# A fused Mamba-2 scan and low-rank mixer on one core: state updates, copies of y and joins become steps of their own, and the order of issue after the sixth pair's second transpose is another one

## The chip, the core and the metric

The kernel runs on 1 core of one Trainium2 chip. The metric is device time in microseconds (us), the median of several executions. Before the change it is 226.42 us (3 runs, 226.41 to 228.46). The profile beside it is one execution, whose span is 224.7 us: from the first to the last instruction of the program that the profiler saw. The 1.7 us between the two lie around the span (start and end of an execution).

The engines are named as in the profile: PE is TensorE's matmul side and PEld its weight loads, DVE is VectorE, ACT is ScalarE, POOL is GpSimd, and SP issues the DMAs. Each engine takes its instructions in the order in which the program has them.

## The reference

Four batches of 768 tokens, eight heads of 32 channels and a state of 16. A scan in chunks of 32 gives y; y of all heads side by side is the input (768 x 256) of a mixer over tokens and channels.

```python
for c in range(nc):                      # chunks of 32 tokens
    cum = np.cumsum(la, axis=-1)
    L = np.exp(cum[:, :, :, None] - cum[:, :, None, :]) * causal
    M = np.einsum('bhin,bhjn->bhij', Cc, Bc) * L
    y_intra = np.einsum('bhij,bhjd->bhid', M, xc)
    y_inter = np.einsum('bhin,bhnd->bhid', Cc, state) * np.exp(cum)[:, :, :, None]
    y[:, :, sl] = y_intra + y_inter
    decay_from_j = np.exp(cum[:, :, -1:] - cum)
    Bx = np.einsum('bhjn,bhjd->bhjnd', Bc, xc) * decay_from_j[..., None, None]
    state = decay_full[:, :, None, None] * state + np.sum(Bx, axis=2)
...
x = y.transpose(0, 2, 1, 3).reshape(B, S, H * D)
h = x.transpose(0, 2, 1) @ U @ V                   # over the tokens, rank 32
u = x + h.transpose(0, 2, 1)
out = u + np.maximum(u @ w_ch1, 0.0) @ w_ch2       # 256 -> 1024 -> 256
```

The weights U, V, w_ch1 and w_ch2 are 64-bit floats in memory; the kernel reads them as words and makes fp32 of them.

## The kernel before

The scan is cut into twelve pairs of 128-token blocks: pair k is block pair k % 3 of batch k // 3. The mixer works per batch b, on halves j of 384 tokens. There is no scheduler: the string PLAN (lines 36 to 73) is the order of issue, word by word, and `follow` (line 859) calls one function for each word. Each function issues its instructions on their engines at once, so the string fixes the order on every engine's queue.

Words of the scan, with the pair's number k:

- `L` loads B, C (three DMAs) and x (two). Words `B X w L` hold their first DMA until the last DVE instruction issued so far has ended (line 864).
- `P` scales B and C (one DVE instruction, tile BC). `T`, twice per pair, gives its four transposes on PE into a bank "w"; the second `T` ends with three ACT copies (tiles T and Cm, lines 484 to 490).
- `g` is the Gram product into all four banks "x" and "z" (line 511); `m` and `M` mask the two x banks and the two z banks (two DVE instructions each, tile M).
- `s` multiplies B and x for the new states into both banks "w" (line 543); `u` makes the running states (up to four DVE instructions, tile S, each needing the one before) and, on POOL, their masked form Sm (line 569).
- `i`, `n`, `j` add up y in the two banks "y" (lines 613 and 635); `y` copies both banks to yT (two ACT copies, line 648); `t` turns yT back to tokens (four transposes into a bank "w" and one copy, line 656).

Words of the mixer, with batch b and half j:

- `p`, `q` project over the tokens (bank "w", tiles pT and ps; lines 679 and 687); `a` adds V's part to yT (line 697); `S` splits u in three parts (tile u: one ACT, two DVE instructions of 128x768).
- `f b.j.m` multiplies column block m of w_ch1 with two of the parts (four matmuls into a bank "x" for even m, "z" for odd m) and scales it on ACT; `e` adds the third part (two matmuls), then the ACT gives the rounded value (line 759); `h` takes the remainder on DVE and so frees the bank. For odd m, `h` goes on with `joined`: one DVE instruction of 128x768 that makes a third operand out of the pair of blocks m-1 and m.
- `d b.j.k.n` is piece n of the second product for token block k of a half: four matmuls of 256 columns, six pieces a block, into one bank whose tag depends on k ("x", "z", "x"; "y" for the last three halves, line 18). Pieces 0 and 1 read the rounded values, 2 and 3 the remainders, 4 and 5 the joined operand. After piece 5 come one more matmul with ps, a DVE addition to ytok and the DMA to the output. Batch 0 has four plain pieces of two fp32 matmuls with two passes each; its first product is `U b.j.m`.
- `c` and `R` convert and split the weights (DVE and ACT).

PSUM holds two banks of each of the four tags "w", "x", "z" and "y". A new use of a bank waits for the instruction that read the old contents. In the traces, operand names are u,w for `f` and `e`, w,words for pieces 0 to 3 of `d`, w2c,words for pieces 4 and 5 and for batch 0, ps,Vs for the last matmul of an output.

Of the kernel before, what the change touches and what calls it, by code (L numbers as in the profile page):

```python
# [10 lines left out]
FP32 = mybir.dt.float32  # L11
# [23 lines left out]
    'b0.0 b0.1 b0.2 x0.0 x0.1 b1.0 b1.1 b1.2 ')  # L35
PLAN = (
# [37 lines left out]


@with_exitstack
def kernel(
# [28 lines left out]
    P = 128  # L106
# [33 lines left out]
            n -= m  # L140

    def bank(tag, *dims):
        t = psum.tile([P, *dims], FP32, tag=tag, name=tag, bufs=BANKS[tag])
        return t

    ctx.enter_context(tc.manual_schedule())

# [72 lines left out]
    w1all = mix.tile([P, NQ, NCB, W], FP32, tag="u", name="w1f", bufs=1)  # L220
    w1f = [w1all[:, c] for c in range(NQ)]
    w2 = [const.tile([P, NM, DM], FP32R, name=f"w2{i}") for i in range(2)]
    weights = []
    w2f, w2b = {}, {}

    def w2c(n, dtype):
# [4 lines left out]
    def words_of(dst):  # L231
        p, i, j = dst.shape
        t = raw.tile([P, 2 * WCOLS], INT32, tag="words", name="words", bufs=NWORDS)
        weights.append((dst, t[:p, :2 * i * j]))
        return t[:p, :2 * i * j]

    def each(parts, *index):
        return [part[index] for part in parts]

    def load_words(dst, src):  # L240

        p, i, j = dst.shape
        t = words_of(dst)
        begin(out=t.rearrange("p (i j) -> p i j", i=i), in_=src)

    U2, V2, w12, w22 = (w.bitcast(INT32) for w in (moe_U, moe_V, moe_w_ch1, moe_w_ch2))
# [4 lines left out]

    def load_v():
        own["UV"] = words_of(UV)
        for q in range(4):
            begin(out=own["UV"][ts(q, Q), 2 * NC * RK:], in_=V2[:, ts(q, 2 * NC * RK)])

# [3 lines left out]

    def load_w(n):
        if n < 2:
            if n == 0:
                own["w"] = words_of(w1f[0])
                weights.pop()
            dst, t = w1f[0][:, :, ts(n, P)], own["w"][:, ts(n, 2 * NCB * P)]
            weights.append((dst, t))
            begin(out=t.rearrange("p (i j) -> p i j", i=NCB),
                  in_=w13[:, :, ts(n, 2 * P)])
        elif n <= NQ:  # L270
            load_words(w1f[n - 1], w13[:, :, ts(n - 1, 2 * quarter)])
        else:
            m = 2 * (n - NQ - 1)
            load_words(w2c(n - NQ - 1, FP32), w22[m * P:(m + 2) * P].rearrange(
                "(m p) d -> p m d", p=P))

    def load(k):
# [271 lines left out]
    def update(k, c=0, n=2):  # L549

        b, q = pairs[k]
        s = st[k]
        if c == 0:
            s["S"] = att.tile([P, 4, 2 * D], FP32, tag="S", name="S")
            s["Sm"] = att.tile([P, 4, 2, D], FP32, tag="Sm", name="Sm", bufs=3)
        own = chunks(k, c, n)
        for i in own:
            j = 4 * q + i
            new, add = s["S"][:, i], s["A"][i % 2][:, i // 2]
            if j == 0:  # L560
                vector.tensor_copy(out=new, in_=add)
            else:
                vector.scalar_tensor_tensor(
                    out=new, in0=st["S", b], scalar=kept[:, b, j - 1, None], in1=add,
                    op0=ALU.mult, op1=ALU.add)
            st["S", b] = new
            st["Sm", b, j + 1] = s["Sm"][:, i].rearrange("p s d -> p (s d)")
        sl = slice(own[0], own[-1] + 1)
        nc.gpsimd.tensor_tensor(  # L569
            out=s["Sm"][:, sl], in0=s["S"][:, sl].rearrange("p i (s d) -> p i s d", s=2),  # L570
            in1=own2[:, b, 4 * q + sl.start:4 * q + sl.stop, :, None].to_broadcast(
                [P, len(own), 2, D]), op=ALU.mult)

    def apart(k):

# [62 lines left out]
                            stop=True, skip_group_check=True)  # L638
                        behind.setdefault(k, []).append(product)

    def yout(k):
        b, q = pairs[k]
        if q == 0 and b:
            yT[b] = mix.tile([P, NCB, S], FP32, tag="yT", name="yT")
            ytok[b] = mix.tile([P, NC, DM], FP32, tag="ytok", name="ytok")
        yp = yT[b][:, :, ts(q, 2 * P)].rearrange("p g (c v i) -> p g c v i", c=2, v=2)
        for p in range(2):
            nc.scalar.copy(out=yp[:, :, :, p], in_=st[k]["y"][p])  # L648

    def ytokening(k, tag="w"):  # L650

# [17 lines left out]
    def mixer(b):  # L669
# [91 lines left out]
        def third(j, m):  # L761
# [2 lines left out]
            vector.scalar_tensor_tensor(  # L764
                out=far[:, m % 2], in0=gs["t", j, m], scalar=0.0,
                in1=near[:, m % 2].bitcast(FP32), op0=ALU.max, op1=ALU.subtract)
            if m % 2:
                joined(near, far, both)

        def down(j, k, n):  # L770

# [18 lines left out]
            if n == pieces - 1:  # L790
# [3 lines left out]
                nc.sync.dma_start(out=out[b, ts(c, P)], in_=o)  # L794

        us, gs, gT = {}, {}, {}
        return SimpleNamespace(p=project, q=parted, a=added, S=split, f=first, e=second, h=third,
                               d=down, U=plain)


# [46 lines left out]
    def ytokens_kept(k):  # L847
        next(turns["O", k])

    scans = dict(P=prep, T=turned, g=gram, s=state, m=lambda k: mask(k, (0, 1)),  # L850
                 M=lambda k: mask(k, (2, 3)), u=update, i=lambda k: inter(k, 0), n=intra,
                 j=lambda k: inter(k, 1), y=yout, t=ytokens, L=load, Q=lambda k, c: prep(k, c, 1),
                 O=ytokens_of, o=ytokens_kept,
                 V=lambda k, c, v: turn(k, c, 1, "wx"[v // 2], vector if v % 2 else None))
# [54 lines left out]
```

## Time and profile before

| | before |
|---|---|
| median of 3 runs | 226.42 us |
| span of the profiled execution | 224.7 us |
| DVE busy | 156.7 us (70%), 329 instructions |
| ACT busy | 114.3 us (51%), 261 instructions |
| POOL busy | 14.3 us (6%), 37 instructions |
| PE: last matmul starts | 220.86 us |
| second transpose of the sixth pair (t5) starts | 64.71 us |
| granted TensorE clock, every slice | full |

All times below are microseconds from the span's start. A busy share of PE is no measure of how fast it goes: a matmul counts as busy until its modelled end, and matmuls overlap. What tells is the distance from the start of one to the start of the next, and so the start of one group to the start of the next.

### The profile page before, as it was taken

To read this page: it belongs to the slowest core of one execution; us is meant where nothing else is said; L and a number is where in the kernel's file an instruction comes from. 1 tells how busy PE (TensorE), PEld (TensorE's weight loads), DVE (VectorE), ACT (ScalarE), POOL (GpSimd) and SP (SyncE) were. 2 spreads that over 40 slices of the span, in tenths; PEclk is the share of its full clock that TensorE was granted. 3 is DMA by queue.
4 is the path that set the end of the run, shared out by engine and by line. 5 is a ranking of instruction groups with operands and counts; after the bars stand their busy time and mean duration, and the time that the engine had idled before them with its cause. 6 is when DMAs were issued, how large, how long until landed. Compare 5 with 4: busy or idle time off the path is not lost.

```text
span 224.7 us, 7010 instructions
## 1 busy us (share of the span) xinstructions
PE 216.0 (96%) x3012; PEld 182.8 (81%) x3012; DVE 156.7 (70%) x329; ACT 114.3 (51%) x261; POOL 14.3 (6%) x37
## 2 busy tenths in 40 slices
PE   7888989999999999999999999999999999999993
PEld 4656655656668898987999898887998999999993
DVE  4776878899998866969717785758437964764921
ACT  3334946856994346334453632475237545655410
POOL 3021010012100000202101000100000000000000
PEclk9999999999999999999999999999999999999999
DMA  6997799788645203600002602000020000100011
GB/s 88 127 111 144 132 130 287 139 163 230 92 65 72 51 23 59 84 23 26 3 26 48 96 0 73 3 3 3 1 71 1 0 0 26 47 0 28 32 38 47
DMA packets 69518, 14.56 MB, mean 65 GB/s; under 512 B 63792, under 2 KB 67696, under 8 KB 69488
## 3 DMA queue, kind: packets, MB, share of 16 engines
q1 hardware_dynamic: 69488, 14.13, 34.6%
q8 instruction: 23, 0.38, 0.7%
q14 instruction: 7, 0.06, 0.1%
HBM read 10.98 MB, written 3.15 MB: 63 GB/s over the span
## 4 chain that ended last, share of the span: by engine, by line
PE 91%; DVE 2%; DMA 2%; SPq 1%; issue 1%; POOL 0%; ACT 0%; POOLq 0%; DVEq 0%
PE x L725 31%; PE z L725 24%; PE y L725 12%; PE y L613 4%; PE y L635 3%; PE w L480 3%; PE x L511 3%; PE w L656 2%; DMA bc<-in_B_dram 2%; PE w L543 2%; PE z L511 2%; PE x L138 1%; SPq L185 1%; PE w L679 1%; PE w L138 1%
## 5 line engine op out<-in xcount | busy, mean ns | idle before, releaser
L159 DVE SCALAR_TENSOR_TENSOR words<-words 128x768 fp32r<-128x768 f32 (+6 forms) x44 | 34.6, 806 | 1.9 <-ACT words L416 0.6
L725 PE MATMUL z<-u,w 128*128 128x384 f32 x144 | 34.0, 350 | 0.0
L725 PE MATMUL x<-u,w 128*128 128x384 f32 x144 | 33.1, 348 | 0.0
L730 ACT ACTIVATE x<-x 128x384 f32<-128x384 f32 (+1 forms) x30 | 13.6, 452 | 25.3 <-PE x L725 25.1
L725 PEld LDWEIGHTS z<-u,w 128*128 128x128 f32 x144 | 24.5, 188 | 1.3 <-DVE words L159 0.2
L725 PEld LDWEIGHTS x<-u,w 128*128 128x128 f32 x144 | 24.0, 188 | 1.3 <-ACT x L730 0.6
L159 DVE SCALAR_TENSOR_TENSOR words<-x,words 128x384 fp32r<-128x384 f32 x24 | 13.2, 555 | 16.4 <-ACT words L759 13.7
L725 PE MATMUL x<-w2c,words 128*128 128x256 f32 x112 | 22.5, 338 | 0.0
L730 ACT ACTIVATE z<-z 128x384 f32<-128x384 f32 (+1 forms) x27 | 12.5, 463 | 14.1 <-PE z L725 13.6
L725 PEld LDWEIGHTS x<-w2c,words 128*128 128x128 f32 x112 | 18.2, 189 | 1.3
L725 PE MATMUL y<-w,words 128*128 128x256 f32 x144 | 19.1, 282 | 0.0
L725 PEld LDWEIGHTS y<-w,words 128*128 128x128 f32 x144 | 18.5, 188 | 0.3 <-DVE ytok L159 0.3
L159 DVE SCALAR_TENSOR_TENSOR words<-z,words 128x384 fp32r<-128x384 f32 x24 | 13.2, 551 | 5.7 <-ACT words L759 5.7
L759 ACT ACTIVATE words<-x 128x384 fp32r<-128x384 f32 x24 | 11.6, 490 | 6.3 <-PE x L725 6.1
L759 ACT ACTIVATE words<-z 128x384 fp32r<-128x384 f32 x24 | 11.6, 491 | 4.9 <-PE z L725 4.8
L648 ACT COPY yT<-y 128x256 f32<-128x256 f32 x24 | 7.8, 384 | 10.9 <-PE y L613 10.7
L569 POOL TENSOR_TENSOR Sm<-S,own 128x256 f32<-128x256 f32 (+1 forms) x12 | 7.7, 644 | 87.5 <-DVE S L159 58.1
L159 DVE SCALAR_TENSOR_TENSOR S<-S,kept,w 128x64 f32<-128x64 f32 x40 | 11.2, 280 | 2.7 <-PE w L543 0.9
L613 PE MATMUL y<-T,Sm 32*64 32x64 f32 x352 | 12.4, 239 | 0.4 <-POOL Sm L569 0.3
L725 PE MATMUL x<-w,words 128*128 128x256 f32 x96 | 12.6, 282 | 0.0
L725 PEld LDWEIGHTS x<-w,words 128*128 128x128 f32 x96 | 12.0, 188 | 0.1
L511 PE MATMUL x<-Cm,T 32*64 32x128 f32 x192 | 11.0, 307 | 1.0 <-ACT Cm L490 0.7
(152 smaller groups left out, 400.5 us busy)
## 6 DMA issues: line engine op xcount, KB each, us to landing
words<-in_moe_w_ch_dram SPq DMA_DIRECT2D x7, 512.0 KB, 6.1
x<-in_x_dram SPq DMA_DIRECT2D x24, 128.0 KB, 3.7
out_dram<-ytok SPq DMA_DIRECT2D x24, 128.0 KB, 1.7
bc<-in_B_dram SPq DMA_DIRECT2D x24, 64.0 KB, 3.7
bc<-in_C_dram SPq DMA_DIRECT2D x12, 128.0 KB, 3.8
words<-in_moe_w_ch_dram SPq DMA_DIRECT2D x2, 256.0 KB, 4.5
words<-in_moe_V_dram SPq DMA_DIRECT2D x4, 48.0 KB, 3.1
words<-in_moe_U_dram SPq DMA_DIRECT2D x1, 192.0 KB, 3.5
```

The source lines that it names most:

```text
L138: nc.tensor.matmul(out=t[:, :m * w].rearrange("p (m i) -> p m i", i=w), lhsT=ident, rhs=ident[:, None, :w].to_broadcast([P, m, w]), start= ...
L159: self.last = call(*args, **kwargs)
L480: nc.tensor.transpose(out=tp[:, i, v], in_=s["BC"][:, i, c + v].rearrange("p h n -> p (h n)"), identity=ident)
L511: nc.tensor.matmul(out=g[r][cols, c], lhsT=s["T"][rows, 0, c, cols], rhs=s["Cm"][rows, :, :, ts(2 * c + p, Q)].rearrange("r v t i -> r v i ...
L543: nc.tensor.matmul(out=s["A"][p][ts(r, Q), v], lhsT=s["BC"][half, 0, v, 2 * r:2 * r + 2].rearrange("p h n -> p (h n)"), rhs=x_sb[k][half, ...
L569: nc.gpsimd.tensor_tensor(out=s["Sm"][:, sl], in0=s["S"][:, sl].rearrange("p i (s d) -> p i s d", s=2), in1=own2[:, b, 4 * q + sl.start:4 ...
L613: product = nc.tensor.matmul(out=y[p][ts(r % 2, H), r // 2, c], lhsT=own[ts(r, Q)], rhs=s["T"][ts(r, Q), 1, :, ts(2 * c + p, Q)].rearrange ...
L635: product = nc.tensor.matmul(out=y[p][ts(i, Q), n, c], lhsT=x_sb[k][half, c, h], rhs=s["M"][half, h // 2, c, h % 2], start=fresh(k, p, [i] ...
L648: nc.scalar.copy(out=yp[:, :, :, p], in_=st[k]["y"][p])
L725: nc.tensor.matmul(out=t, lhsT=lhsT, rhs=rhs, start=start, stop=True, skip_group_check=True)
L730: nc.scalar.activation(t, t, AF.Copy, scale=1.0 + EPS)
L759: nc.scalar.activation(gs[j, m // 2][0][:, m % 2], t, AF.Relu, scale=NEAR)
```

## The change

Three functions are cut. `yout` copies one bank of y at a time (`y k.p`). `update` takes one block of the pair at a time (`u k.c`); the POOL instruction is still one for the pair and comes with the second. `joined` is called by a word of its own, `J b.j.i`, no longer by `h`. The list of converted weights becomes a table by number, so that loads could be in any order. No instruction is added or taken away on any engine.

```diff
@@ update
-        sl = slice(own[0], own[-1] + 1)
+        if c + n < 2:
+            return
+        sl = slice(0, own[-1] + 1)
@@ yout
-    def yout(k):
+    def yout(k, p):
...
-        for p in range(2):
-            nc.scalar.copy(out=yp[:, :, :, p], in_=st[k]["y"][p])
+        nc.scalar.copy(out=yp[:, :, :, p], in_=st[k]["y"][p])
@@ third
-            if m % 2:
-                joined(near, far, both)
+
+        def fourth(j, n):
+
+            joined(*gs[j, n])
```

PLAN is the same up to `t5 m6` (pieces of `u` and `y` stand side by side there). What follows is in another order. Four places of it, the order of before above that of after:

```diff
-    'y5 U0.0.7 c8 U0.0.5 t5 m6 n6 R3 c9 c9 P8 c8 p1 R7 g7 m7 L9 i6 M7 T8 T8 c8 c8 q1 d0.0.2.0 '
-    'd0.0.2.1 U0.1.5 a1.1 R1 d0.0.2.2 d0.0.2.3 a1.0 d0.0.1.0 R3 d0.0.1.1 d0.0.1.2 d0.0.0.0 d0.0.0.1 '
+    'U0.0.5 t5 m6 c8 U0.1.5 L10 R5 P8 c8 T8 p1 n6 c8 i6 g7 m7 R1 M7 j6 T8 c9 q1 c9 d0.1.2.0 d0.1.2.1 '
+    'd0.0.1.0 d0.1.2.2 R7 d0.0.1.1 R3 a1.0 y6.1 d0.1.2.3 d0.0.0.0 R3 a1.1 S1.0 P10 d0.0.0.1 d0.0.0.2 '
...
-    'd0.1.1.2 d0.1.1.3 e1.0.4 e1.0.5 d0.1.2.1 d0.1.2.2 h1.0.4 h1.0.5 R6 d0.1.2.3 s8 j6 g8 y6 u8 s9 '
-    'm8 n7 i7 S1.1 f1.1.0 f1.1.2 j7 y7 u9 M8 t6 R5 e1.1.0 h1.1.0 n8 i8 T9 T9 t7 R5 d1.0.1.0 '
+    'h1.0.5 s7 u7.0 f1.0.4 d0.0.2.3 u7.1 f1.0.1 e1.0.4 J1.0.3 h1.0.4 f1.0.0 d0.1.1.2 L9 e1.0.1 '
+    'd0.1.0.0 y6.0 d0.1.0.1 R7 e1.0.0 h1.0.0 d0.1.1.3 h1.0.1 J1.0.2 d0.1.0.2 d0.1.0.3 n7 s8 i7 L11 '
+    'P9 u8.0 g8 M8 j7 m8 T9 S1.1 d1.0.1.0 d1.0.1.1 J1.0.0 T9 d1.0.2.0 f1.1.1 f1.1.0 y7.0 d1.0.2.1 '
...
-    'd1.1.0.5 d1.1.2.4 d1.1.2.5 d1.1.1.4 d1.1.1.5 T10 g9 m9 T10 T11 T11 M9 i9 n9 g10 m10 M10 j9 y9 '
-    's11 u11 i10 g11 m11 M11 n10 f2.0.4 a2.1 f2.0.3 f2.0.2 e2.0.4 h2.0.4 e2.0.3 e2.0.2 f2.0.7 '
-    'f2.0.6 h2.0.2 h2.0.3 f2.0.0 f2.0.1 e2.0.0 e2.0.7 e2.0.1 h2.0.0 h2.0.1 j10 y10 t9 e2.0.6 h2.0.6 '
-    'h2.0.7 f2.0.5 i11 n11 e2.0.5 h2.0.5 d2.0.1.0 d2.0.0.0 d2.0.0.1 d2.0.0.2 d2.0.0.3 d2.0.1.1 '
+    'd1.1.2.1 d1.1.2.2 d1.1.2.3 d1.1.0.4 d1.1.1.4 d1.1.2.4 d1.1.2.5 d1.1.1.5 d1.1.0.5 s10 g9 u10.0 '
+    'u10.1 T10 m9 T10 T11 M9 T11 i9 n9 g10 m10 j9 y9.0 M10 s11 y9.1 i10 u11.0 g11 M11 u11.1 m11 n10 '
+    'f2.0.7 a2.1 f2.0.2 e2.0.7 h2.0.7 f2.0.0 f2.0.3 e2.0.2 j10 h2.0.2 t9 e2.0.0 e2.0.3 y10.1 f2.0.4 '
+    'f2.0.5 h2.0.0 h2.0.3 f2.0.6 y10.0 f2.0.1 e2.0.5 e2.0.4 J2.0.1 e2.0.6 e2.0.1 i11 h2.0.5 h2.0.1 '
+    'h2.0.6 n11 t10 d2.0.1.0 d2.0.2.0 d2.0.2.1 d2.0.2.2 h2.0.4 S2.1 d2.0.1.1 J2.0.3 d2.0.2.3 f2.1.1 '
...
-    'h2.1.1 e2.1.2 h2.1.2 h2.1.3 f2.1.4 p3 e2.1.4 f2.1.5 f2.1.6 h2.1.4 e2.1.5 h2.1.5 q3 f2.1.7 '
+    'f2.1.3 d2.0.0.3 f2.1.6 e2.1.5 t11 e2.1.3 e2.1.6 h2.1.6 h2.1.3 J2.1.1 p3 d2.0.0.4 q3 f2.1.7 '
```

More of the change, by code (lines that the diff above doesn't have):

```diff
@@ L142, in bank @@
     def bank(tag, *dims):
-        t = psum.tile([P, *dims], FP32, tag=tag, name=tag, bufs=BANKS[tag])
-        return t
+        return psum.tile([P, *dims], FP32, tag=tag, name=tag, bufs=BANKS[tag])
     ctx.enter_context(tc.manual_schedule())
@@ L222 @@
     w2 = [const.tile([P, NM, DM], FP32R, name=f"w2{i}") for i in range(2)]
-    weights = []
+    weights = {}
     w2f, w2b = {}, {}
@@ L233, in words_of @@
         t = raw.tile([P, 2 * WCOLS], INT32, tag="words", name="words", bufs=NWORDS)
-        weights.append((dst, t[:p, :2 * i * j]))
         return t[:p, :2 * i * j]
@@ L238, in each, with load_words @@
         return [part[index] for part in parts]
-    def load_words(dst, src):
+    def load_words(n, dst, src):
         p, i, j = dst.shape
         t = words_of(dst)
+        weights[n] = dst, t
         begin(out=t.rearrange("p (i j) -> p i j", i=i), in_=src)
@@ L253, in load_v @@
         own["UV"] = words_of(UV)
+        weights[1] = UV, own["UV"]
         for q in range(4):
@@ L262, in load_w @@
         if n < 2:
-            if n == 0:
+            if "w" not in own:
                 own["w"] = words_of(w1f[0])
-                weights.pop()
             dst, t = w1f[0][:, :, ts(n, P)], own["w"][:, ts(n, 2 * NCB * P)]
-            weights.append((dst, t))
+            weights[2 * n] = dst, t
             begin(out=t.rearrange("p (i j) -> p i j", i=NCB),
@@ L270, in load_w @@
         elif n <= NQ:
-            load_words(w1f[n - 1], w13[:, :, ts(n - 1, 2 * quarter)])
+            load_words(n + 1, w1f[n - 1], w13[:, :, ts(n - 1, 2 * quarter)])
         else:
             m = 2 * (n - NQ - 1)
-            load_words(w2c(n - NQ - 1, FP32), w22[m * P:(m + 2) * P].rearrange(
+            load_words(n + 1, w2c(n - NQ - 1, FP32), w22[m * P:(m + 2) * P].rearrange(
                 "(m p) d -> p m d", p=P))
@@ L567, in update @@
             st["Sm", b, j + 1] = s["Sm"][:, i].rearrange("p s d -> p (s d)")
-        sl = slice(own[0], own[-1] + 1)
+        if c + n < 2:
+            return
+        sl = slice(0, own[-1] + 1)
         nc.gpsimd.tensor_tensor(
             out=s["Sm"][:, sl], in0=s["S"][:, sl].rearrange("p i (s d) -> p i s d", s=2),
-            in1=own2[:, b, 4 * q + sl.start:4 * q + sl.stop, :, None].to_broadcast(
-                [P, len(own), 2, D]), op=ALU.mult)
+            in1=own2[:, b, 4 * q:4 * q + sl.stop, :, None].to_broadcast(
+                [P, sl.stop, 2, D]), op=ALU.mult)
     def apart(k):
@@ L639, in intra @@
                         behind.setdefault(k, []).append(product)
-    def yout(k):
+    def yout(k, p):
         b, q = pairs[k]
-        if q == 0 and b:
+        if b not in yT:
             yT[b] = mix.tile([P, NCB, S], FP32, tag="yT", name="yT")
@@ L796, in mixer @@
         us, gs, gT = {}, {}, {}
-        return SimpleNamespace(p=project, q=parted, a=added, S=split, f=first, e=second, h=third,
+        return SimpleNamespace(p=project, q=parted, a=added, S=split, f=first, e=second, h=third, J=fourth,
                                d=down, U=plain)
@@ L850 @@
     scans = dict(P=prep, T=turned, g=gram, s=state, m=lambda k: mask(k, (0, 1)),
-                 M=lambda k: mask(k, (2, 3)), u=update, i=lambda k: inter(k, 0), n=intra,
+                 M=lambda k: mask(k, (2, 3)), u=lambda k, c: update(k, c, 1), i=lambda k: inter(k, 0), n=intra,
                  j=lambda k: inter(k, 1), y=yout, t=ytokens, L=load, Q=lambda k, c: prep(k, c, 1),
```

55 rows, old and new, of the table PLAN are left out of this document.

## The prediction

> **What bounds the kernel now.** I read the engines' busy times, the chain of waits by engine, and the timeline of PE, DVE and ACT from 64.71 us on, where the two orders part.
>
> ```profile
> PE 216.0 (96%) x3012; PEld 182.8 (81%) x3012; DVE 156.7 (70%) x329; ACT 114.3 (51%) x261; POOL 14.3 (6%) x37
> ...
> PE 91%; DVE 2%; DMA 2%; SPq 1%; issue 1%; POOL 0%; ACT 0%; POOLq 0%; DVEq 0%
> ```
>
> PE bounds it. As no instruction comes or goes, only time in which PE advances slower than it can is to be had. Its best rate, from PE's timeline:
>
> ```profile
> 130.21 1.58 PE L725 MATMUL z<-w,words 128*128 128x256 f32 x12
> 131.64 2.53 PE L725 MATMUL x<-w,words 128*128 128x256 f32 x20
> 134.00 0.40 PE L725 MATMUL x<-w2c,words 128*128 128x256 f32 x2
> ```
>
> 32 matmuls in 3.79 us: 0.118 each. In the same way 16 of 384 columns start from 191.42 to 194.19: 0.174 each. The small ones in these rows:
>
> ```profile
> 139.80 0.86 PE L635 MATMUL y<-M,x 64*32 64x64 f32 x64
> 140.59 0.35 PE L511 MATMUL x<-Cm,T 32*64 32x128 f32 x2
> ...
> 141.18 0.47 PE L613 MATMUL y<-T,Sm 32*64 32x64 f32 x12
> 141.58 0.53 PE L543 MATMUL w<-x,BC 64*32 64x64 f32 x24
> 142.15 0.57 PE L613 MATMUL y<-T,Sm 32*64 32x64 f32 x8
> ```
>
> `n` costs 0.79, `g` 0.59 and `i` or `j` 0.40 (start to next start); `s` 0.36 (101.21 to 101.57).
>
> By these prices I went through PE's groups from 64.71 on. Between 107.4 and 137.2 and from 156.3 to 211.6 they stand at their price. The losses: 0.2 at the start (an addition of V's part at 71.53 waits for ps, on DVE 71.05 to 71.48); 0.6 in stage 1 (100.8 to 107.4: `g8` 0.72, the mixed `s9`, `n7` 1.38, first products 1.59 for 1.48 and others); 1.7 in stage 2 (137.2 to 145.6, with its transposes: `g9` 1.08, `s11` 0.57, `j10` with `g11` 1.47 for 0.93, first products 0.80); 0.8 behind it (145.6 to 156.3: 6.74 for 6.26 from 145.57, 1.41 for 1.13 from 153.15, 0.46 for 0.35 at 155.79); 0.2 at 211.67. Together about 3.2 us, all that can go: 223.2 us.
>
> **Pieces.** `u`, `y` and `J` issue what was issued before, in smaller words: 0. POOL's one instruction a pair waits for the pair's last `u` as it did.
>
> **Start.** After puts `U0.1.5` ahead of `T8`, and `P8` ahead of `c9` on DVE; ps is then ready about 1 us before `a1.0` reads it. The wait goes: -0.2. `c9`'s DVE instruction (0.69) ends some 0.7 us before its reader; no new wait.
>
> **Loads.** `L9` moves from about 68 to 96 us, where its first DMA is held until the DVE instruction of `h1.0.4` ends, about 95.9. From the load at 87.09: its three issues take 0.39, 0.57 and 0.57 and the last lands 4.65 after the first issue, so about 100.7. `P9`, the DVE instruction that needs it, is due at about 102.1. Slack 1.4 us: 0. `L10` is earlier. Output DMAs on SP behind the hold come from work that PE does later anyway: 0.
>
> **Stage 1.** Counted from the last ps matmul of batch 0: ps matmul and change of tile 0.39, `n7` to 1.18, `s8` 1.54, `i7` 1.88, `g8` 2.48, `j7` 2.91, two transposes 3.13. DVE masks from 2.75; the first z bank is free at 3.18, when `d1.0.1.0` wants it: 0.05 late. Masks and the two parts of u:
>
> ```profile
> 138.67 0.76 DVE L159 TENSOR_TENSOR M<-x,causal 128x256 int32<-128x256 int32 x2 [0.86 <-PE z L511]
> 139.34 0.74 DVE L159 TENSOR_TENSOR M<-z,causal 128x256 int32<-128x256 int32 x2
> ...
> 142.77 0.90 DVE L159 SCALAR_TENSOR_TENSOR S<-S,kept,w 128x64 f32<-128x64 f32 x3
> 143.72 0.76 DVE L159 TENSOR_TENSOR M<-x,causal 128x256 int32<-128x256 int32 x2
> ```
>
> A mask starts 0.335 after the one before it, four take 1.41; an S 0.30, 768 columns 0.88 (busy 0.96). Masks end at 4.09, u is split at 5.05, wanted at 5.2; the pieces of `d1.0` that after puts here cover it. The chain goes on through `J1.0.0` and conversions to 8.65, wanted at 8.8. So 0.1 of the 0.6 stays: -0.5. These nine DVE instructions have next to no slack: 0.1 us more on them is 0.1 on PE.
>
> [...] Here the second mask starts before the first ends (0.335 against 0.41). With each at its full duration the chain would be an estimated 0.7 longer and the -0.5 gone; the rows speak for mine.
>
> **Stage 2.** Here `s10` and `u10` stand now at the head, where before's `T10 g9` stood; before had them among second products. Counted from the last ps matmul (137.06): the ytok addition starts at 0.32, as before (137.38); four S instructions follow, 0.76 to 1.96. They read both banks w. `T10` wants these: it waits to 1.7, the other half to 2.0. What follows then lies later than before: ACT's copy of T at 2.4
>
> ```profile
> 139.05 0.59 ACT L484 COPY T<-w 128x512 f32<-128x512 f32 x1 [4.48 <-PE w L480]
> 139.53 0.84 ACT L490 ACTIVATE Cm<-w,slot 128x256 f32<-128x256 f32 x2
> ```
>
> (before 139.05, so 1.99), `g10` 3.85, state 4.85 (four small groups behind it), `g11` ends at 6.9 (6.56), the first product of batch 2 starts at 7.7 (144.41, so 7.35). But the stage holds 0.36 more of PE's work, which is gone elsewhere. The same loss of 1.7: 0. Its bounds: all of `T10`'s wait of 1.2 comes on top (+1.2), or the masks `M9` fill the ACT copies' time (-0.4). I stay at 0, where the rows put the first product.
>
> **Behind stage 2.** The loss came from DVE: a remainder that frees a bank stood behind `joined` (149.96, 153.65) and a copy of ytok (154.53). With `J` moved behind the remainders, each bank is free 0.9 earlier; walking PE's order by the prices above I find no first product waiting: of 0.8, 0.2 stays (changes of tile): -0.6. What is late next is `J`: `J2.0.1` is read by pieces 4 and 5 alone, which come over 5 us behind. If those were not behind, -0.6 would be 0.
>
> **End.** The wait at 211.67 is for the y bank of an output just ended (DVE addition at 211.55). After lets `d3.1.1.0` take one that ended five groups earlier: -0.15. It costs 0.2 if that addition is queued behind `J3.1.0`.
>
> **New.** The second projection `q1` now has only two pieces of c9's word (0.47) between it and its ACT copy (0.40), and other places are tight in the same way: +0.3 (0 to 0.6, by such a copy's duration).
>
> Sum: -0.2 -0.5 +0 -0.6 -0.15 +0.3 = -1.15. The span goes from 224.7 to 223.55, and with the 1.7 us around it (226.42 - 224.7) to 225.3.
>
> **Rivals.**
> *No gain, 226.4.* `s10` and `u10` in stage 2 are exposed, +1.2, and the rest comes as summed: 225.3 + 1.2 = 226.5. For it: `T10`'s wait for the w banks cannot be hidden by what I see between. Against it: ACT's copies and the masks left PE idle there already, 0.5 us at `g9` and 0.5 at `j10` with `g11`. 0.22.
>
> *Larger gain, 223.6.* Stage 2 loses its chains too, -1.7 + 0.0: 225.3 - 1.7. For it: u10 is split from `M9`, so DVE has no three S between masks (142.77). Against it: ACT's chain T, Cm, T, Cm is unchanged, 139.05 to 141.59. 0.12. [...]
>
> *Slower, 227.2.* `L9` lands late, `P9` stands on DVE, and behind it `u8`, the masks and u, hence `T9` and all first products of the half. From a landing over 5.0 us after the third issue (3.58 in the row, plus 1.4) it costs one to one; over 6.1 the kernel is slower than before, over 8.4 by 1%. Rows: at most 4.3 between 53 and 125 us, but 6.9 at 47 us, while weights load too: 225.3 + 1.9. 0.08.
>
> *DVE at full durations, 225.9.* Each DVE instruction of stage 1 starts only when the one before has ended: nine of them, 0.08 each (0.41 - 0.335, 0.96 - 0.88), 0.7 late less the slack. Against it: every row of two masks. 0.02.
>
> *It doesn't do what it says.* If the order on PE stayed, nothing would move: 226.4. Every group from 65 us on must stand in another order. 0.02.
>
> **How the numbers follow.** Forecast 0.54, with its own range 224.4 to 226.0. A measurement here can tell 1% (2.26 us), so faster is below 224.16 and slower above 228.68. Below: most of the larger gain and the forecast's low edge, 0.14. Above: the late load beyond 8.4 us, and stage 2 and the load together, 0.08. Within: 0.78. The range runs to 223.5 (larger gain) and 227.2 (the late load at 6.9).
>
> **What would show it.** Stage 1: `n7` to the first piece of `d1.0.1` in about 3.2 us; PE waiting there for DVE's BC tile shows the late load. Stage 2: from the last ps matmul to the first u,w 7.7 us; 8.9 is the no-gain rival, 6.5 the larger gain. Behind it: no wait of a first product for DVE. Up to 64.7 us all as before; if the start moves by more than 0.2 there, the comparison falls. I am wrong if PE waits in the stretches that now stand at their price, 107 to 137 and 156 to 211: after reorders these as well, and I count nothing there.

## The result and the profile after

The changed kernel takes 225.43 us (median of 23 runs, 224.37 to 229.16), before in the same runs 226.5. The ratio is 0.9941, 95% interval 0.9917 to 0.9965: 0.6% faster. Predicted were 225.3 us and 0.995.

In some executions, of the old order and the new, PE's granted clock is lower for a while ahead of the change (0.50 from 36.51 to 39.92 us in the first profile of the changed kernel; 0.91 on average from 20 to 40 us there and in the old order with the joins later), so I compare stretches of PE from t5 on (below) and take the profile of an execution of the changed kernel at full clock throughout: span 223.2 us, against 224.7. Its line numbers are 3 to 6 higher, as its source is longer. Its page:

```profile
PE 213.4 (96%) x3012; PEld 182.2 (82%) x3012; DVE 155.7 (70%) x329; ACT 113.7 (51%) x261; POOL 13.7 (6%) x37
...
PE 84%; SPq 8%; DMA 4%; issue 2%; DVE 2%; DVEq 0%
```

The counts stand as they were, and busy times are within 5%. The chain's share of PE is lower because, in the first 20 us, which the change does not touch, it runs over the issues on SP in this execution (15.29, a load of C) and over PE in the other; that says nothing of the change. What tells is when PE reaches the same work, from the starts of groups in PE's timeline. Moved work is put back at its own price: `j6` (0.43) now lies before stage 1, `s10` (0.38) in stage 2, the transposes of `t10` (0.41) behind it.

| stretch of PE, us | before | changed | moved work put back | gain or loss | predicted |
|---|---|---|---|---|---|
| t5 to the last ps matmul of batch 0 | 36.11 | 36.37 | -0.43 | -0.17 | -0.2 |
| to the last ps matmul of batch 1 (stage 1 is in it) | 36.25 | 34.89 | +0.81 | -0.55 | -0.5 |
| to matmul 2378 of the program, the first behind a2.1 (stage 2) | 8.51 | 9.44 | -0.38 | +0.55 | 0 |
| to the first w,words of batch 2 | 10.67 | 10.43 | -0.41 | -0.65 | -0.6 |
| to the last matmul | 64.62 | 63.80 | +0.41 | -0.41 | +0.15 |
| to the end of the span | 3.87 | 3.54 | | -0.33 | none |

The sum is -1.56, as the spans say; predicted was -1.15, with which the rows ahead of the last one, -1.23, are to be compared. The last row has the same instructions in both. Among the kernels below that end alike it goes with the order ahead of stage 2 (the head): 3.87 to 3.89 with the old head, 3.53 or 3.54 with the new one, whatever the tail. Why is open.

The stage 2 row is one execution. Five other traces with this same stage 2 have 9.15 to 10.00 there (below), so its +0.55 lies between +0.26 and +1.11.

Stage 2 in PE's timeline of the changed kernel:

```profile
135.96 0.28 PE L729 MATMUL x<-ps,Vs 128*128 128x256 f32 x1
136.17 0.46 PE L546 MATMUL w<-x,BC 64*32 64x64 f32 x32
...
137.90 1.06 PE L483 MATMUL w<-ident,BC 128*128 128x128 f32 x8 [0.35 <-DVE S L162]
...
141.10 0.38 PE L546 MATMUL w<-x,BC 64*32 64x64 f32 x14
141.94 0.32 PE L546 MATMUL w<-x,BC 64*32 64x64 f32 x10 [0.47 <-issue]
...
143.17 0.86 PE L640 MATMUL y<-M,x 64*32 64x64 f32 x64
143.96 0.96 PE L729 MATMUL z<-u,w 128*128 128x384 f32 x4
144.76 0.37 PE L701 MATMUL x<-Vs,ps 128*128 128x384 f32 x1
144.97 0.34 PE L701 MATMUL z<-Vs,ps 128*128 128x384 f32 x1
145.40 0.87 PE L729 MATMUL x<-u,w 128*128 128x384 f32 x4
```

`T10` waits for the S instructions, as predicted (1.94 after the last ps matmul; the sum had 1.7). The first u,w starts 8.00 after that ps matmul (143.96), between the 7.7 of the sum and the 8.9 of the no-gain rival. Two stops come that were not foreseen: `s11` stops after its 14th matmul, and the product behind a2.1 starts 0.43 after it where 0.18 is the price; "issue" means that PE waited for nothing that the profile shows. `s11` took 0.56 before and 1.10 now. Stage 1 in DVE's timeline, and the PE rows that wait for it:

```profile
101.91 0.68 DVE L162 TENSOR_TENSOR BC<-bc,F 128x512 f32<-128x512 f32 x1
102.73 0.60 DVE L162 SCALAR_TENSOR_TENSOR S<-S,kept,w 128x64 f32<-128x64 f32 x2
103.66 0.76 DVE L162 TENSOR_TENSOR M<-z,causal 128x256 int32<-128x256 int32 x2 [0.33 <-PE z L514]
104.33 0.74 DVE L162 TENSOR_TENSOR M<-x,causal 128x256 int32<-128x256 int32 x2
105.00 0.95 DVE L162 TENSOR_TENSOR u<-yT,u 128x768 fp32r<-128x768 f32 x1
```
```profile
104.23 1.18 PE L729 MATMUL z<-w,words 128*128 128x256 f32 x8
105.25 0.38 PE L483 MATMUL w<-ident,BC 128*128 128x128 f32 x2
105.39 0.72 PE L729 MATMUL x<-w,words 128*128 128x256 f32 x4
105.95 0.86 PE L729 MATMUL z<-u,w 128*128 128x384 f32 x4
```

The first piece of `d1.0` starts 3.17 after the last ps matmul of batch 0 (101.06; the sum had 3.18), between the masks, and the first product when the first part of u is there (105.00 + 0.95).

### The profile page after: what moved, and what is told of

Same layout as the page of the kernel before. It is cut to its first block, busy times and chain, and to the rows that moved or that the text cites. A ratio compares the mean times of both kernels' runs of the same rounds, so it can differ in the third digit from the quotient of the medians.

```text
span 226.7 us, 7014 instructions
## 1 busy us (share of the span) xinstructions
PE 215.2 (95%) x3012; PEld 183.1 (81%) x3012; DVE 155.8 (69%) x329; ACT 113.6 (50%) x261; POOL 13.9 (6%) x37
## 4 chain that ended last, share of the span: by engine, by line
PE 87%; SPq 4%; DMA 4%; DVE 2%; issue 1%; ACT 0%; POOL 0%; DVEq 0%; POOLq 0%
PE x L728 31%; PE z L728 23%; PE y L728 12%; DMA bc<-in_B_dram 4%; PE y L617 4%; SPq L187 4%; PE y L639 4%; PE w L482 2%; PE w L659 2%; PE x L513 2%; PE w L545 2%; PE z L513 1%; PE w L682 1%; DVE S L161 1%; PE x L700 1%
## 5 line engine op out<-in xcount | busy, mean ns | idle before, releaser
L161 DVE SCALAR_TENSOR_TENSOR words<-words 128x768 fp32r<-128x768 f32 (+6 forms) x44 | 33.7, 800 | 1.5 <-ACT words L420 0.8
L728 PE MATMUL z<-u,w 128*128 128x384 f32 x144 | 33.5, 344 | 0.0
L728 PEld LDWEIGHTS x<-u,w 128*128 128x128 f32 x144 | 24.6, 188 | 1.2 <-issue 0.7
L728 PE MATMUL x<-w2c,words 128*128 128x256 f32 x112 | 23.0, 338 | 0.0
L728 PE MATMUL y<-w,words 128*128 128x256 f32 x144 | 19.6, 281 | 0.0
L573 POOL TENSOR_TENSOR Sm<-S,own 128x256 f32<-128x256 f32 (+1 forms) x12 | 8.8, 734 | 96.4 <-DVE S L161 96.4
L728 PE MATMUL x<-w,words 128*128 128x256 f32 x96 | 13.6, 283 | 0.0
L728 PE MATMUL x<-yT,w1f 128*128 128x384 f32 x32 | 12.8, 542 | 0.1
L161 DVE TENSOR_TENSOR BC<-bc,F 128x512 f32<-128x512 f32 (+2 forms) x18 | 9.0, 512 | 5.5 <-DMA bc<-in_B_dram 4.1
L486 ACT COPY T<-w 128x512 f32<-128x512 f32 (+1 forms) x10 | 5.7, 568 | 14.1 <-PE w L482 14.1
```

The lines of the kernel that those rows point to most:

```text
L161: self.last = call(*args, **kwargs)
L486: nc.scalar.copy(out=s["T"][:, :, c:c + n], in_=tp)
L573: nc.gpsimd.tensor_tensor(out=s["Sm"][:, sl], in0=s["S"][:, sl].rearrange("p i (s d) -> p i s d", s=2), in1=own2[:, b, 4 * q:4 * q + sl.st ...
L728: nc.tensor.matmul(out=t, lhsT=lhsT, rhs=rhs, start=start, stop=True, skip_group_check=True)
```

## The experiments

All kernels are built from the changed one, and only PLAN differs unless said. "t5 to the last matmul" is 156.15 us before and 154.93 changed.

**The changed kernel again**, for the profile above.

> The changed kernel once more, for a profile at full clock; nothing is altered. Ratio to the kernel before 0.994 to 0.996 (the sum of the prediction is -1.15 us, 0.995). Step by step against before, as lost time on PE over the best rate: start 0.2 gone; stage 1 loses 0.1 to 0.2 of the 0.6; stage 2 loses 1.7 (the sum) or more; behind it 0.2 of 0.8. In the profile already seen PE stood twice in stage 2 for about 0.5 us each with nothing that it waited for; if these stops belong to the order they stand there again, if they are chance they do not.

Ratio 0.9991 (0.995 to 1.0032); its 12 executions spread from 224.36 to 228.93, so it does not add to the first. From t5 to the last matmul the first profile of the changed kernel took 155.51 and this one 154.93; the only stretch that differs is the product behind a2.1 (0.56 later there). The stop in `s11` stands at the same matmul in both, and in the four other traces below that keep this stage 2 (joins at once, the late load, the masks twice, and the small matmuls at the end), so it belongs to the order. Its length does not: PE idles 0.18 to 0.48 there, and stage 2 takes 10.00, 9.44, 9.69, 9.51, 9.69 and 9.15 in the six.

**Old and new halves.** The two orders have done the same work at the last ps matmul of batch 1, but for `s10` and `u10`. So heads and tails can be exchanged.

```diff
 new head, old tail
 d1.0.0.0 j8 y8.0 t7 d1.0.0.1
+s10
 d1.0.0.2 d1.0.0.3
+u10.0 u10.1
...
 d1.1.1.5 d1.1.0.5
-s10 g9 u10.0 u10.1 T10 m9 T10 T11 M9 T11 i9 n9
+T10 g9 m9 T10 T11 T11 M9 i9 n9
...
 old head, new tail
 d1.1.1.4 d1.1.1.5
-T10 g9 m9 T10 T11 T11 M9 i9 n9
+g9 T10 m9 T10 T11 M9 T11 i9 n9
...
```

> The changed order up to the last output of batch 1, then the old order; s10 and u10 among the second products, as in the old order. By the sum it keeps the start and stage 1 (-0.2, -0.5) and most of the new costs (+0.3): -0.4 against before, ratio 0.998. Rival: the gain comes from the tail alone (fewer waits behind stage 2), ratio 1.000. Rival: the head carries it all, 0.995.

> The old order up to the last output of batch 1, with s10 and u10 inside it, then the changed order without them. By the sum: -0.6 behind stage 2, -0.15 at the end, ratio 0.997; if u10 was exposed in stage 2 of the changed kernel, another -0.4 to -0.8 is gained here, 0.994.

Ratios 1.0128 (1.0092 to 1.0164) and 1.0016 (0.9978 to 1.0055); t5 to the last matmul 157.08 and 155.37 (before 156.15). The ratio of the second (old head, new tail) does not show its gain of 0.78: the times of single executions spread by several us. Stretch by stretch they add up:

| | t5 to batch 0 | to batch 1 | to matmul 2378 | to first w,words | to last matmul |
|---|---|---|---|---|---|
| before | 36.11 | 36.25 | 8.51 | 10.67 | 64.62 |
| changed | 36.37 | 34.89 | 9.44 | 10.43 | 63.80 |
| old head, new tail | 36.10 | 36.23 | 8.73 | 10.47 | 63.84 |
| new head, old tail | 36.37 | 36.52 | 8.51 | 11.04 | 64.64 |

Each stretch keeps the time of its own order, within 0.05, but for three places. With the new head and the old tail the head is 1.63 longer for 0.38 of work: where I put `s10` it waits for the w banks (0.36), and a first product behind its S instructions waits for a remainder (its start is 0.60 late). So that ratio says nothing of the change; its 11.04 has a stop, told below. Stage 2 of the new order without `s10` takes 8.73, with it 9.44: `s10` costs 0.33 more there than its work (0.04 to 0.89 by the six traces), and the order itself 0.22.

**s10 ahead**, the new order at both ends:

```diff
 d1.0.0.1
+s10
 d1.0.0.2 d1.0.0.3
+u10.0 u10.1
...
-s10 g9 u10.0 u10.1 T10 m9
+g9 T10 m9
```

> The changed kernel with s10 and u10 moved ahead, among the pieces of d1.0.0, where the old order had them about. If u10 is exposed in stage 2 (its four S instructions hold both banks w and T10 waits), 0.5 to 0.8 us is gained against the changed kernel: ratio 0.991 to 0.993, and the first product of batch 2 starts under 7.4 us after the last ps matmul of batch 1, with 0.38 less of work. If ACT's chain of T and Cm copies sets the end of stage 2 whatever stands ahead, the time is that of the changed kernel, 0.995.

Ratio 1.0003 (0.9971 to 1.0035). The head is longer as above (36.52), stage 2 is 8.74 for 9.44. The first u,w comes 7.58 after the last ps matmul, not under 7.4: `g9` now waits itself, for the bank of the output just ended (1.31 for 0.59). So one wait took the place of the other, and the 0.33 is gained in stage 2 but not the 0.5 to 0.8 that I expected. No stop stands in `s11` (0.57).

**What the stops are.** The DMA view has a queue q8 of the kind "instruction". Its line for 139 to 142 us of the changed kernel (kind, packets, MB, share of 16 engines) is

```profile
q8 instruction: 1, 0.02, 1.9%
```

One transfer of 16 KB. By the trace there are 23 of them for 3012 matmuls with as many weight loads, 131 matmuls a transfer, and the two stops stand 128 matmuls apart. I took the transfers for pieces of PE's instructions. I shifted the pieces against the order with small matmuls ahead of the first Gram product (`E40.3`, in a second kernel `E72.3`), and in a third kernel gave PE nothing but small matmuls behind the last output (`E768.0`):

```diff
+    def tiny(n, tag):
+        two = [bank("wxzy"[tag], 4 * P) for v in range(2)]
+        for i in range(n):
+            half = ts(i % 2, H)
+            nc.tensor.matmul(out=two[i % 2][ts(i // 2 % 4, Q), :H], lhsT=ident[half, :Q],
+                             rhs=ident[half, :H], start=True, stop=True, skip_group_check=True)
...
-                 v=lambda n: spread())
+                 v=lambda n: spread(), E=tiny)
...
 Q1.2 Q1.1
+E40.3
 g0 m0
...
 d3.1.0.4 d3.1.0.5
+E768.0
```

> The changed kernel with 40 small matmuls more (64x32, on ident, into two free y banks, never read) ahead of the first Gram product, where PE waits 0.66 us anyway. Theory: PE's instructions come in pieces of 16 KB on a DMA queue of their own, 128 matmuls with their weight loads a piece, and PE stops where the next piece isn't there. Then the stop of 0.7 us that stood after the 14th matmul of s11 (matmul 2250 of the program) stands again at matmul 2250, which now is 40 matmuls earlier in the order, in the Gram product g10, some 1.3 to 1.5 us after the end of a transfer of 16 KB; s11 takes 0.4 to 0.6. Rival: s11 waits for something of its own (a bank, x, ACT's copies): its 1.1 us stays. Time within 0.5 us of the changed kernel, either way.

> The same with 72 small matmuls: by the theory the stop at matmul 2250 would fall into n9, near its 50th matmul, and the next, at 2378, behind g11; both come earlier against the pieces before them, so the stops are shorter or gone (0 to 0.5 us in all, from 1.0). Stage 2 then takes 0.5 less, and the kernel 0 to 0.5 less than the changed kernel. Rival as before: s11 still takes 1.1.

> The changed kernel and behind it 768 small matmuls (64x32, on ident, into two free w banks, never read) that wait for nothing. At the 12.4 ns each that intra shows they take 9.5 us. By the theory of the instruction pieces, six pieces of 128 have to come, each 1.0 to 1.1 us after the one before it is begun, 1.0 to 1.5 in transfer and 1.3 to 1.5 until it runs: 3.4 to 4.0 us a piece, so 19 to 24 us in all, in bursts of 128 with stops between.

An fp32 matmul is two in the trace, so the shifts are 80 and 144, and the tail has 1536. PE's timeline of the tail's start:

```profile
219.07 1.52 PE L866 MATMUL w<-ident 64*32 64x64 f32 x133
220.84 1.47 PE L866 MATMUL w<-ident 64*32 64x64 f32 x128 [0.26 <-issue]
224.57 1.47 PE L866 MATMUL w<-ident 64*32 64x64 f32 x128 [2.26 <-issue]
228.03 2.04 PE L866 MATMUL w<-ident 64*32 64x64 f32 x128 [1.99 <-issue]
231.48 2.04 PE L866 MATMUL w<-ident 64*32 64x64 f32 x128 [1.42 <-issue]
```

Twelve bursts take 39 us, with stops between; all but the first and the last have exactly 128. From the second on they start 3.45 or 3.46 apart eight times, 3.73 once and 4.00 once. At the rate of `n` the 1536 would take 19 us; I had expected 19 to 24 for six pieces. Behind each of these bursts a transfer starts 1.0 to 1.6 after the burst does and takes 0.9 to 1.2, and the next burst starts 1.2 to 1.5 behind its end; from 224 to 259 us, where ten bursts start, q8 has 10 packets, 0.16 MB. The granted clock was 0.53 from 224 to 259 us, so the 2.04 us of a burst are no price; what counts is that PE stops ahead of each. In the shifted kernels, phase_40 first:

```profile
145.69 0.43 PE L546 MATMUL w<-x,BC 64*32 64x64 f32 x24
...
147.26 0.29 PE L514 MATMUL z<-Cm,T 32*64 32x128 f32 x1
147.89 0.29 PE L514 MATMUL z<-Cm,T 32*64 32x128 f32 x1 [0.34 <-issue]
```
```profile
153.47 0.78 PE L640 MATMUL y<-M,x 64*32 64x64 f32 x54
155.74 0.44 PE L640 MATMUL y<-M,x 64*32 64x64 f32 x10 [1.49 <-issue]
156.11 1.65 PE L729 MATMUL z<-u,w 128*128 128x384 f32 x4
```

`s11` takes 0.56 and 0.53, and the stops stand in `g11` and `n10`. Counted from the first matmul of the trace, with the last 16 KB ahead of each:

| kernel | stop before matmul | remainder by 128 | transfer | PE goes on | behind its end |
|---|---|---|---|---|---|
| changed | 2250 | 74 | 139.71 to 140.64 | 141.94 | 1.30 |
| changed | 2378 | 74 | 143.07 to 143.99 | 145.40 | 1.41 |
| new head, old tail | 2379 | 75 | 146.67 to 148.08 | 149.54 | 1.46 |
| phase_40 | 2378 | 74 | 145.19 to 146.56 | 147.89 | 1.33 |
| phase_72 | 2506 | 74 | 152.88 to 154.28 | 155.74 | 1.46 |

The rival, that `s11` waits for something of its own, is out: the stop moves through the order with the count and stays 1.30 to 1.46 behind the end of a transfer. Which piece binds I had wrong: in phase_40 I expected the stop at matmul 2250 (in `g10`), but its piece had come 3.46 earlier, and the stop stands at the next one. In phase_72 I expected shorter stops and a stage 2 that is 0.5 shorter; one stop is 1.49 long, and the stage takes 12.02 for 9.44. My expectation of the times was wrong too: the ratios are 1.017 (1.011 to 1.0231) and 1.0389 (1.0329 to 1.0448). Up to t5 the shifted kernels took 4.6 and 10.1 us longer, in the first 64 us, where the small matmuls are thickest; some of it is a lowered clock (0.97 and 0.89 on average there), and how much of it is pieces I have not separated. From t5 on they took 155.21 and 158.02.

**The joins.** One kernel gives the old order the deferred joins, one takes them from the new order:

```diff
 the old order, joins later
 h2.0.2 h2.0.3
-J2.0.1
...
 h2.0.0 h2.0.1
-J2.0.0
...
 h2.0.6 h2.0.7
-J2.0.3
...
 h2.0.5
-J2.0.2
+J2.0.1 J2.0.0 J2.0.3 J2.0.2
...
 the new order, joins at once
 h2.0.3
+J2.0.1
...
 e2.0.4
-J2.0.1
...
 h2.0.1
+J2.0.0
 h2.0.6
+J2.0.3
...
 h2.0.4
+J2.0.2
 S2.1 d2.0.1.1
-J2.0.3
 d2.0.2.3 f2.1.1 f2.1.0
-J2.0.0
 d2.0.1.2 j11 e2.1.0
-J2.0.2
```

> The old order with one change: the four joins of the first half of batch 2 stand together behind the last remainder (h2.0.5), not each behind its pair. By the prediction's term for the joins the first products no longer wait for remainders: between the first u,w and the first w,words of batch 2, 0.3 to 0.6 less than the 11.83 of before (144.41 to 156.24), ratio 0.998. Rival: what is saved there comes back, since S2.1 and the pieces 4 and 5 now wait for four joins in a row (3.5 us of DVE): ratio 1.000 or above.

> The changed kernel with the four joins of the first half of batch 2 directly behind the second remainder of their pair, as the old order has them; all else as changed. By the prediction the remainders that free banks stand 0.9 later on DVE: first products wait as before, +0.3 to +0.7 against the changed kernel (0.997 of before), seen between the first u,w and the first w,words of batch 2. Rival: the joins had nothing to do with that loss (instruction pieces had), the time is the changed kernel's, 0.994.

Ratios 1.0042 (1.0003 to 1.0081) and 1.0034 (0.9995 to 1.0073). From matmul 2378 to the first w,words: 10.67 before and 10.66 with the joins later; 10.43 changed and 10.48 with the joins at once. There they do nothing. What waits there in the old order, in its timeline of weight loads and in its list of their waits (total, times, longest):

```profile
147.73 0.30 PEld L725 LDWEIGHTS x<-u,w 128*128 128x128 f32 x2 [0.19 <-ACT x L730]
151.06 0.30 PEld L725 LDWEIGHTS x<-u,w 128*128 128x128 f32 x2 [0.19 <-ACT x L730]
```
```profile
PEld z L725 <- DVE words L159: 0.2, 1, 0.2
```

The first two are `e` words that stand close behind their `f` and wait until ACT has scaled the bank; the third is a first product that waits for a remainder. Against a matmul every 0.174 (384 columns) or 0.107 (transposes), the starts in this stretch come 1.01 late in all before: 0.14 at each of these `e` words, 0.20 at the remainder, 0.11 or less at each other place. With the joins later it is 1.00, at the same places. In the changed kernel, with the old head and new tail, with the joins at once and with the transposes first it is 0.39, and none of these three is there. So the loss goes with the order of these words; no run moves them alone. Behind the first w,words the joins count: 65.20 for 64.62 in the old order, 65.76 for 63.80 in the new one, where the waits of PE between 150 and 165 us are

```profile
PE z L729 <- DVE u L162: 0.8, 1, 0.8
PE x L729 <- DVE words L162: 0.5, 1, 0.5
```

With four joins ahead of them, the last remainder and u of the next half come late.

**Transposes first**, in search of a shorter stage 2:

```diff
 d1.1.0.3
+s10
 J1.1.3
+u10.0 u10.1
 S2.0
...
-s10 g9 u10.0 u10.1 T10 m9 T10 T11 M9 T11 i9
+T10 T10 T11 T11 g9 m9 M9 i9
```

> The changed kernel with s10 and u10 between the pieces of d1.1 (u10 behind J1.1.3), and stage 2 opened by the eight transposes instead of g9. Waits on banks and ACT's copies then allow the first product of batch 2 some 7.1 us after the last ps matmul of batch 1 (same order as now: 8.0), and matmul 2378 at 8.15. By the theory of the instruction pieces matmul 2378 comes no sooner than 3.45 behind matmul 2250, at 8.6 or later (9.4 now). Against that, s10 among wide matmuls costs 0.6 where it now costs 0.4. Time 0.2 to 0.5 under the changed kernel, ratio 0.992 to 0.993; if the pieces did not bind, 0.990.

Ratio 0.9923 (0.9886 to 0.996), beside 0.9941 of the changed kernel: not told apart; t5 to the last matmul 154.94, the same. Matmul 2378 comes 8.78 after the last ps matmul (8.6 or later was said), 1.49 behind the end of its transfer, as behind a stop; but no stop stands ahead of it, so this run does not show that the piece binds. PE now waits for the masks of `n9` (0.35 ahead of it, 0.58 in it) in place of `T10`'s wait. Of the 0.66 saved in stage 2, 0.38 is the work of `s10`, and the head pays 0.59 (35.48 for 34.89). Nothing beat the changed kernel clearly.

**The slack of stage 1**: a load later, and DVE longer.

```diff
 the late load
 d0.1.1.2
-L9
 e1.0.1
...
 h1.0.0
+L9
...
 the masks twice
 M8 j7 m8
+m8
 T9
```

> The changed kernel with L9 behind h1.0.0: its first DMA is held until that DVE instruction ends, 3.8 us later (99.83 for 96.0 in the profile). It tests the price of the late load: by the prediction (slack 1.4, then one to one, since P9 stands ahead of u8, the masks and u on DVE) the kernel gets 2.4 slower; with the landing that the profile now shows (97.07 + 3.9 = 101.0, P9 at 101.9, slack 0.9) 2.9. PE would wait between g8 or T9 and the first pieces of d1.0. Rival: other work covers part of it, under 1.5.

> The changed kernel with the two masks m8 done a second time right behind (two more DVE instructions, 0.67 us, the same values). By the prediction the chain on DVE from the masks over u and the join to the conversions has 0.05 to 0.15 slack, so +0.5 to +0.6 on PE, seen as a wait of the first u,w of the second half of batch 1. Rival: pieces of d1.0 cover it, 0.

The late load: ratio 1.0104 (1.0059 to 1.015). `P9` on DVE waits for the load, and PE's `T9` for the S instructions of `u8`, which stand behind `P9`:

```profile
106.78 0.69 DVE L162 TENSOR_TENSOR BC<-bc,F 128x512 f32<-128x512 f32 x1 [2.77 <-DMA bc<-in_B_dram]
```
```profile
108.13 0.66 PE L483 MATMUL w<-ident,BC 128*128 128x128 f32 x2 [2.21 <-DVE S L162]
```

From t5, `P9` comes 2.9 later, as said, but the stretch to the last ps matmul of batch 1 is 3.40 longer (38.29). In that stretch the granted clock was 0.57 from 108.1 to 111.6 us (below): the eight matmuls of 256 columns from 108.46 take 1.85 to the next start, 1.02 in the changed kernel. The masks: ratio 0.9962 (0.9921 to 1.0003), that stretch 35.35, so +0.46 for 0.67 of DVE; the slack was 0.2.

## Why the prediction was right

The time, its sign and its size came out, and most of the places where PE gains are those that were named. But two terms were wrong by more than 0.5, stage 2 (+0.55 for 0) and the last stretch (-0.41 for +0.15), and covered each other. That the sum came out so close is in part luck.

- **The bound.** The losses listed add up to 3.5 us (0.2 + 0.6 + 1.7 + 0.8 + 0.2), not to 3.2; no term of the sum hangs on it.
- **Pieces, start.** As summed: -0.17 for -0.2.
- **Loads.** The last third of `L9` was issued at 97.07 and landed 3.9 later, 101.0, where I had 100.7; `P9` came at 101.9. The slack was 0.9, not 1.4, and the price, one to one, was too low: the late load costs 3.40 for 2.9, and in that run the granted clock was 0.57 from 108.1 to 111.6 us.
- **Stage 1.** As summed, -0.55 for -0.5, with the chain that was named; doubling two masks shows that it binds (+0.46 on PE for 0.67 on DVE). The second of two masks starts 0.33 to 0.34 after the first here too (103.66, 0.76 for both), so the 0.7 of full durations did not come.
- **Stage 2.** The step that failed: "the same loss of 1.7: 0". It is +0.55. The wait of `T10` was there, 0.24 longer than summed; the new order without `s10` is 0.22 slower than the old one on the same work; and the stop in `s11` with the one behind a2.1, 0.8 together, I had not seen as possible at all. Against the order whose `s10` stands ahead, 0.33 of that is left; there PE waits at `g9` instead.
- **Behind stage 2.** The size is right (-0.65 for -0.6), the cause is not. I put the loss down to remainders behind `joined`; the joins alone change nothing there (10.66 for 10.67). The old order loses in `e` words close behind their `f`, for ACT (0.28), at one remainder (0.20), and in small amounts elsewhere. In the new order the joins must stand later, for what comes behind: at once, they cost 1.96 there.
- **New and end.** The +0.3 of new small costs did not come: the second projection loses as much as before, at other places. The wait at 211.67 went, with the slow start behind it: -0.28, predicted -0.15. The other 0.13 of the last stretch is not traced to a place, and the 0.33 at the end of the span had no term and no explanation.
- **Rivals.** "No gain" and "larger gain" had stage 2 move; it moved by 0.55, to the side of the first, for a reason that neither named. The late load did not occur; in the run that makes it, it cost 3.40 us. Idle weight loads were no measure of room here: they idle 41.0 of 223.2 us now, 41.9 of 224.7 before, and the gain came out of waits while idle loads fell by 0.9 only.

## What to carry to other kernels

In an order with many small matmuls, count them. Here PE stopped after 128 of them, again and again in small_tail and ahead of matmuls 2250 and 2378 in the changed stage 2; there, and from burst to burst, the next 128 started 3.45 to 4.00 us after the ones before. What a shorter chain on DVE or ACT buys in such a stretch, no run showed. One fast stretch of 128 alone did not stop PE: in the order before, the 128 matmuls from 2122 on start within 2.23 us, with no stop behind them. The stops inside a group are named "issue" (0.47 us in `s11`, 0.34 in phase_40, 1.49 in phase_72); count matmuls from the start of the program to see whether such a stop keeps its place. And that a term has the right size does not show that its cause is right: the edit of one part alone (joins later) shows in one run that it was not.

## What the hardware showed unexpectedly

PE went through the matmuls of small_tail in bursts of 128, from the second on 3.45 to 4.00 us apart, at a granted clock of 0.53 from 224 to 259 us. At full clock matmul 2378 started 3.46 us after matmul 2250 in the profile of the changed kernel shown above (141.94 and 145.40) and 4.00 in its first profile (144.92 and 148.92); by the price of `n` 128 take an estimated 1.6 (12.4 ns each). The count of q8's 16 KB transfers goes with the count of matmuls: 23 for 3012, 24 for 3092 (phase_40), 25 for 3156 (phase_72). PE was idle for up to 0.63 us at such a place in stage 2 of the changed kernel (ahead of matmul 2378 in the first profile), and for 1.49 in phase_72. That PE stops because the next of these transfers has not come is my reading of the counts and of the times in the table; no run shows it more directly.

Behind some waits of PE the granted clock was lower: 0.57 from 108.1 to 111.6 us in the late load, with the wait of 2.21 up to 108.13; 0.54 from 155.7 to 159.2 in phase_72, with the stop of 1.49 up to 155.74; 0.50 from 36.51 to 39.92 in the first profile of the changed kernel, with a wait of 2.36 from 32.15 on. Busy time of PE, granted clock, DMA share and GB/s by windows of phase_72:

```profile
150.00:155.70 5.70, 4.03 (x202) 0.98 0.02 3
155.70:159.20 3.50, 3.46 (x20) 0.54 0.02 5
159.20:162.00 2.80, 2.80 (x31) 1.00 0.00 0
```

Matmuls of 384 columns start every 0.32 to 0.36 there, for 0.174. After the waits of 0.8 and 0.5 with the joins at once the clock stayed at 1.00 (155 to 162 us). What lowers the clock, no run shows.
